# Windowed attention plus MLP on one core: GpSimd issues in written order, loads stand behind rstd and eight blocks ahead, and eight more q/k tiles are turned by DMA

## The chip, the core and the metric

The kernel runs on one core of a Trainium2 chip. The metric is the device time of one execution in microseconds. Three runs of the kernel before took 316.97, 318.75 and 320.42 us, median 318.75 us. One further execution was profiled. The core has TensorE (PE; its weight loads are shown apart as PEld), VectorE (DVE), ScalarE (ACT), GpSimd (POOL) and SyncE (SP), and 16 DMA engines. POOL and SP start DMAs from queues of their own: POOL's are the ones whose descriptors are made in software, and they can change the type on the way (fp32 to fp16 here); SP's also do transposes.

## What is computed

The reference, cut to what matters (8 batches, 8 heads, 576 positions, head size 64; model width 512, hidden width 2048):

```python
rel = pos[:, None] - pos[None, :]
bias = slopes[:, None, None] * (-np.abs(rel))[None]
mask = (rel >= 0) & (rel < 128)
scores = np.where(mask, scale * q @ k.T + bias, -1e9)
attn = softmax(scores)
x = (attn @ v).transpose(0, 2, 1, 3).reshape(B, S, 512)
xn = (x - mean(x)) / sqrt(var(x) + 1e-6) * g_ln
out = x + np.maximum(xn @ w_ch1, 0) @ w_ch2
```

## The kernel before, in words

**Blocks.** The 8 batches are taken as 4 pairs. Pair p has nine blocks of 128 positions: blocks 0 to 7 alternate between the two batches (four blocks of 128 positions each), and block 8 holds the 64 last positions of both. Through the whole kernel they are counted as n = 9p + block, 0 to 35. So block 4 of the second pair (p = 1) is n = 13. A block sees its own keys and those of the same batch one step back (two blocks back in n).

**Turns.** q and k come from memory with positions on the partitions, and the scores need the head dimension there. One *turn* (`turn`, L303 to L338) does that for q and k of two neighbouring blocks, or of block 8 alone: index i = block // 2 runs over 0 to 4. For pairs 0 to 2 PE does it, with 64 small transposes of 64x64 (32 for i = 4, L301) into the two score banks (or, for a few early turns, other banks), and DVE and ACT copy q and k out (L333, L334, L338). For pair 3 four DMA transposes on the SP queue do it (two for i = 4, L322). `turn_at(n)` places a turn three blocks ahead of its block when PE does it and four blocks ahead when DMA does it, and it is called with n + 1 at the end of step n.

After a PE turn both score banks hold leftovers (`junk`). The next scores into each bank then compute whole 64x128 tiles for one of the two head rows (`seen`, L395 on) where half of a tile would do.

**Steps.** From block 8 on, the step of block n does: the masks and values (probabilities times v, L489) of n, then the scores of n + 2 and their exponential on ACT (L436, L445), the mask products of later blocks on DVE (L456), the statistics of block n (`stats`: L586 and L587 on DVE, then two GpSimd instructions L541 and L544 that give rstd), a turn, and the normalised block xc on DVE (`normal`, L528), which waits for rstd. xc is turned into xT by a DMA transpose on the SP queue (L536). The first eight blocks get their statistics and centring another way, on DVE and PE alone.

**MLP.** Blocks are put in groups: six of two blocks, then six of four. `mlp1` (L732, ReLU on ACT L748 or DVE L740) and `mlp2` (L765 for the small groups; L831 for the big ones, which use a Strassen-like scheme with combinations on DVE, L800, L189) run on PE, and the steps of the blocks are woven between their units by hand (`weave_at`). The output adds are L909 and L849, the stores L924 and L928 on the SP queue.

**Loads.** q, k, v and the weights are loaded by GpSimd (L155, L196, L237, L234, L247), from one list in block order. For a PE turn (L237) a batch's q or k comes in one DMA with two positions side by side, so a run holds 128 elements; for a DMA turn (L234) k comes in one DMA per batch and q in two (even and odd positions apart), and a run holds 64 elements. `load_until(place[n + AHEAD])` lets the list run up to block n + 6 at the first half of the values of block n. There are four buffers each for raw q, raw k, turned q and turned k, ten for v.

**Order.** PE, SP, ACT and DVE run in the order in which the code writes their instructions (`manual_schedule`). GpSimd is not in that list before: its instructions are put in order by a scheduler at build time. In the program built that way the loads stand further ahead than six blocks at times, and loads stand in front of rstd, for instance q and k of blocks 20 and 21 around the rstd of block 9.

Of the kernel before, what the change touches and what calls it, by code (L numbers as in the profile page):

```python
# [26 lines left out]
FAST, HURRIED = 6, 11  # L27

NV = 10
BY_DMA_TURN = 3  # L30
AHEAD = 6

FIRST_GROUPS, FIRST = 2, 4

BY_DMA = SEEN = 8
# [24 lines left out]
def kernel(  # L60
# [146 lines left out]

    raw = {}

    def by_dma(p):  # L210
        return p >= BY_DMA_TURN

    def load_qk(src, tag, p, i):

        n = min(P, S - i * P)
        t = raw_pool.tile([P, H, 2, D], FP16, tag=tag, name=tag)
        raw[tag, p, i] = t
        if by_dma(p):
            t = raw[tag, p, i] = t.rearrange("p h r d -> p (h r d)").rearrange(
                "p (b h d) -> p b h d", b=2, h=H  # L220
            )
            for b in range(2):
                rows = src[2 * p + b, :, i * P : i * P + n, :]
                if i == 4:
                    parts = [(t[b * n : (b + 1) * n, 0], rows)]
                elif tag == "k":
                    parts = [(t[:, b], rows)]
                else:
                    rows = rows.rearrange("h (c r) d -> h r c d", r=2)
                    parts = [  # L230
                        (t[r * HALF : (r + 1) * HALF, b], rows[:, r]) for r in range(2)
                    ]
                for dst, part in parts:
                    nc.gpsimd.dma_start(out=dst, in_=part.rearrange("h p d -> p h d"))  # L234
            return
        for b in range(2):
            nc.gpsimd.dma_start(  # L237
                out=t[b * n // 2 : (b + 1) * n // 2],
                in_=src[2 * p + b, :, i * P : i * P + n, :].rearrange(
                    "h (c r) d -> c h r d", r=2  # L240
                ),
            )
# [10 lines left out]
    order = [(p, blk) for p in range(NPAIR) for blk in range(NSLOT)]  # L253
    w1s, w2s = ([(f, c) for c in range(4)] for f in (load_w1, load_w2))
    weights = {3: w1s + w2s[:2], 5: w2s[2:]}
    loads, place = [], []
# [21 lines left out]
    def warm(n):  # L278

        if n:  # L280
            ps = ps_mm.tile([P, 4 * P], FP32, tag="mm", name="ps_warm")
        for _ in range(n):
            nc.tensor.matmul(ps, ones[:, 0:P], ones, start=True, stop=True)  # L283
# [7 lines left out]
    def transposed(tag, p, i, ps):  # L291


        st = raw.pop((tag, p, i))
        for hp in range(HP):
            for r in range(2):
                for b, dst in enumerate(ps):
                    rows = slice(b * HALF, (b + 1) * HALF)
                    for j in range(2):
                        cols = slice(j * HALF, (j + 1) * HALF)  # L300
                        nc.tensor.transpose(  # L301
                            dst[cols, r, hp, :],
                            st[rows, 2 * hp + j, r, :],  # L303
                            iden[rows, rows],
                        )

    def turn(p, i, in_sc=False, copies=(nc.vector.tensor_copy, nc.scalar.copy)):

        k = keys_tile("k", p, i)
        q = queries(p, i) if i < 4 else keys_tile("q", p, i)
        if by_dma(p):
            for tag, dst in (("q", q), ("k", k)):
                src = raw.pop((tag, p, i))
                for b in range(2 if i < 4 else 1):
                    t = dst[:, b]
                    if tag == "q" and i < 4:  # L320
                        t = turned["q", p, i][:, b].rearrange("p h r c -> p h (r c)")
                    nc.sync.dma_start_transpose(  # L322
                        out=t, in_=src[:, b].rearrange("p h d -> p (h d)")
                    )
            return
        ps = [bank(b if in_sc else None) for b in range(2)]
        if i < 4:
            transposed("q", p, i, [t[:, 0] for t in ps])
            if p == 0 and i == 1:
                warm(3)  # L330
            transposed("k", p, i, [t[:, 1] for t in ps])
            for b, copy in enumerate(copies):
                copy(out=q[:, b], in_=ps[b][:, 0])  # L333
                copy(out=k[:, b].rearrange("p h (c r) -> p r h c", r=2), in_=ps[b][:, 1])  # L334
        else:
            for tag, t, dst, copy in zip("qk", ps, (q, k), copies):
                transposed(tag, p, i, [t[:, 0]])
                copy(out=dst[:, 0].rearrange("p h (c r) -> p r h c", r=2), in_=t[:, 0])  # L338

    def bank(sc=None):  # L340
        if sc is None:
            return ps_mm.tile([P, 2, 2, HP, HALF], FP16, tag="mm", name="ps_tr")
        junk[sc] = True
        return ps_sc[sc][:, 0].bitcast(FP16).rearrange(
            "p (t r h c) -> p t r h c", t=2, r=2, h=HP
        )

    def queries(p, i):
        if by_dma(p):
            t = turned_pool.tile([P, 2, HP, 2, HALF], FP16, tag="q", name="q")  # L350
            turned["q", p, i] = t
            return t
        t = turned_pool.tile([P, 2, 2, HP, HALF], FP16, tag="q", name="q")
        turned["q", p, i] = t.rearrange("p b r h c -> p b h r c")
        return t

    def keys_tile(tag, p, i):
        t = turned_pool.tile([P, 2, HP, P], FP16, tag=tag, name=tag)
        turned[tag, p, i] = t
        return t  # L360
# [259 lines left out]
    for g, size in enumerate(GROUPS):  # L620
        n = sum(GROUPS[:g])
# [3 lines left out]
    count = len(order)  # L625
# [5 lines left out]
    def scores_step(n):  # L631
        return [(scores,) + order[n]]

    def values_steps(n):
        p, blk = order[n]
        ahead = place[min(n + AHEAD, count - 1)]
        return [
            [(load_until, ahead), (masks, p, blk), (values, p, blk, 0)],
            [(values, p, blk, 1), (centre, p, blk)],
        ]  # L640

    def x_step(n, copy=nc.vector.tensor_copy):
# [6 lines left out]
    def masks_of(n, *halves):  # L649
        return [(masks,) + order[n] + halves]  # L650

    def warm_step(n):
        return [[(warm, n)]]


    steps = warm_step(11) + [[(turn_first,)]] + warm_step(3)
# [27 lines left out]
    def turn_at(n):  # L684
        ahead = [m for m in (n + 3, n + 4) if m < count and order[m][1] % 2 == 0]
        return [
            f
            for m in ahead
            if by_dma(order[m][0]) == (m == n + 4)
            for f in turn_step(m, True)  # L690
        ]

    steps.append(turn_at(8))
    for n in range(8, count):
        first_half, second_half = values_steps(n)
        step = first_half + second_half[:1]
        if n + 1 < count and order[n + 1][1] == T:
            step += [(scores_tail, order[n][0])]
        if n + 2 < count:
            step += scores_step(n + 2)  # L700
        steps.append(step)
        to_mask = [m for t in (n + 1, n + 2) if t < count for m in masks_of(t)]
        turns = [turn_at(n + 1)] if n + 1 < count else []
        if n == HURRIED:
            steps += [[(normal, n - 1)], to_mask + [(stats, n)], [(normal, n)], *turns]
        else:
            steps += [to_mask + [(stats, n)], *turns]
            if n != HURRIED - 1:
                steps.append([(normal, n)])
    combined = combine_w2()  # L710
# [236 lines left out]
    decay(m_tail, 4)  # L947
    load_until(place[3])
    engine = mybir.EngineType
    with tc.manual_schedule(engines={engine.PE, engine.SP}):  # L950
        with tc.manual_schedule(engines={engine.Activation, engine.DVE}):
            advance_to(first)
            weave_at(mlp1(0, (0, 1)), 2, 7, 8, 9, 13)
            weave_at(mlp1(1), 2, 8, 12)
            weave_at(mlp2(0, ((0, 8), (8, 12), (12, NFB))), 0, 1, 3, 4, 4, 5)
            weave_at(mlp2(1), 0, 1, 2, 3, 4, 6, 6)
            weave_at(mlp1(2), 0, 3, 3, 6, 8, 11)
            weave_at(mlp2(2), 0, 2, 4, 6, 7)


            weave_at(mlp1(3, (9, 10, 11)), 8, 8, 12, 15)
            weave_at(mlp2(3), 0, 1, 1, 3, 4, 4, 6, 6)
            weave_at(mlp1(4), 0, 4, 8, 10, 10, 14)
            weave_at(mlp2(4), 0, 2, 2, 5, 5, 7, also=(1, 4, 6))
            weave_at(mlp1(5), 0, 5, 5, 8, 10, 12, also=(3, 6, 9))
            weave_at(mlp2(5), 0, 1, 2, 4, 6, 7)
            ring += [ps_mm.tile([P, DM], FP32, tag="mm", name="ps_r") for _ in range(4)]
            for g in range(6, len(GROUPS)):
                weave_at(
                    mlp1(g), 0, 2, 5, 7, 8, 10, 13, 15, also=(1, 4) if g == 6 else ()  # L970
                )
                weave_at(fast_mlp2(g), 1, 3, 6, 7, 7, 10, 12, 13)
# [31 lines left out]
```

## Time and profile before

| | |
|---|---|
| runs, median (lowest to highest) | 318.75 us (316.97 to 320.42) |
| the profiled execution: its time | 317.64 us |
| its span | 315.8 us |
| granted PE clock, mean | 0.996 |
| busy: PE, DVE, ACT, POOL | 304.8, 228.8, 179.7, 125.8 us |
| PE transposes of q and k, L301, mean of one | 195 ns (overlapping) |
| copies of a turn: q and k on DVE (L333, L334) | 418 and 725 ns |
| copies of a turn: q and k on ACT (L333, L334) | 587 and 743 ns |
| load by POOL for a PE turn (L237), issue of one | 692 ns, x4 a turn |
| load by POOL for a DMA turn (L234), issue of one | q 708 ns x4, k 888 ns x2 |
| DMA transpose on SP (L322, L536), issue of one | 1.2 us |
| packets in the software queue, share of 16 engines | 89280, 74.1% |

The time is the span plus what lies around it (1.84 us here). Busy time of an engine is the union of its instructions; small PE instructions overlap, so a row's mean times its count is more than what it adds to PE. A line number is that of the kernel before. In the prediction's excerpts each row of the timeline gives the start, the length, the engine, the line, the operation and the count, and in brackets the idle time of the engine before it with what ended it.

### The profile page before, as it was taken

Reading aid. Unit: us, or ns where it says so; the run is one execution under the profiler, and the core shown is the slowest. Engines: PE = TensorE matmul, PEld = TensorE weight load, DVE = VectorE, ACT = ScalarE, POOL = GpSimd, SP = SyncE. Lnnn points to the kernel's source line nnn. Section 1 sums busy time; section 2 is a strip of 40 time slices with the busy share of each in tenths; the row PEclk is TensorE's granted clock in tenths of the full one; section 3 lists DMA queues with packets and bytes.
Section 4 is the critical chain, followed back from the end, with each engine's and each line's share of the span. In section 5 each row is a group of like instructions: output and inputs, shape, how many; then the busy total and the mean of one; then the engine's idle time right before and its main releaser. Section 6 shows DMA issues by size and latency. Waiting matters only on the chain.

```text
span 315.8 us, 9932 instructions
## 1 busy us (share of the span) xinstructions
PE 304.8 (97%) x4195; PEld 205.2 (65%) x4195; DVE 228.8 (72%) x547; ACT 179.7 (57%) x311; POOL 125.8 (40%) x198
## 2 busy tenths in 40 slices
PE   8989999999999999999999999999999999999994
PEld 2468655756757567554885488558756875784583
DVE  2788877877578698758994889479948994761363
ACT  6588765667667557378348832772487247305600
POOL 8932758666254356575254672140001001100001
PEclk9999999999999999999999999999999999999998
DMA  9999999999997999599959995892457144015004
GB/s 111 172 206 198 191 141 179 198 134 144 105 119 96 91 114 141 60 166 46 69 63 166 159 119 69 133 153 52 94 97 114 18 85 85 19 37 114 0 2 134
DMA packets 121087, 34.68 MB, mean 110 GB/s; under 512 B 112049, under 2 KB 116657, under 8 KB 121042
## 3 DMA queue, kind: packets, MB, share of 16 engines
q0 software_dynamic: 89280, 18.49, 74.1%
q1 hardware_dynamic: 31362, 15.09, 25.0%
q8 instruction: 33, 0.54, 0.7%
q10 hardware_dynamic: 400, 0.46, 0.5%
q14 instruction: 12, 0.10, 0.1%
HBM read 36.90 MB, written 9.44 MB: 147 GB/s over the span
## 4 chain that ended last, share of the span: by engine, by line
PE 84%; DVE 6%; ACT 4%; issue 2%; DMA 1%; POOL 1%; DVEq 0%; ACTq 0%
PE ps_r L732 27%; PE ps_r L831 23%; PE ps_m L732 10%; PE ps_m L765 9%; PE ps_sc L436 4%; PE ps_sc L301 3%; PE ps_r L489 3%; PE ps_warm L283 2%; PE ps_pv L489 2%; ACT probs L445 2%; DMA q<-in_q_dram 1%; DVE x L498 1%; DVE o L909 1%; DVE probs L456 1%; DVE o L849 1%
## 5 line engine op out<-in xcount | busy, mean ns | idle before, releaser
L732 PEld LDWEIGHTS <-w1g 128*128 128x128 f16 x640 | 60.4, 98 | 50.1 <-issue 1.9
L732 PE MATMUL ps_r<-xT,w1g 128*128 128x512 f16 x384 | 85.1, 379 | 0.0
L445 ACT ACTIVATE probs<-ps_sc 128x1024 f16<-128x1024 f32 x56 | 54.2, 1026 | 51.1 <-PE ps_sc L436 51.1
L748 ACT ACTIVATE ht<-ps_r 128x512 f16<-128x512 f32 x96 | 56.2, 600 | 31.6 <-PE ps_r L732 31.5
L541 POOL TENSOR_TENSOR rstd<-moments,powers 128x1 f32<-128x1 f32 x28 | 6.9, 245 | 99.1 <-DVE moments L587 98.1
L765 PE MATMUL ps_m<-w,ht 128*128 128x512 f16 x192 | 46.0, 380 | 0.0
L247 POOL DMA_DIRECT2D vx<-in_v_dram x40 | 34.5, 876 | 26.3 <-PE ps_r L489 9.0
L831 PE MATMUL ps_r<-w,ht 128*128 128x256 f16 x384 | 44.1, 273 | 0.0
L456 DVE TENSOR_TENSOR probs<-probs,m 128x1024 f16<-128x1024 f16 x56 | 37.5, 688 | 7.2 <-ACT probs L445 7.0
L831 PEld LDWEIGHTS <-ht 128*128 128x128 f16 x384 | 37.1, 98 | 4.8
L748 ACT ACTIVATE ht<-ps_m 128x256 f16<-128x256 f32 x91 | 33.3, 390 | 8.8 <-PE ps_m L732 6.2
L732 PE MATMUL ps_m<-xT,w1g 128*128 128x256 f16 x256 | 31.3, 273 | 1.9 <-DVE o L909 0.7
L765 PEld LDWEIGHTS <-ht 128*128 128x128 f16 x192 | 17.0, 98 | 17.5
L237 POOL DMA_DIRECT2D q<-in_q_dram x30 | 20.6, 693 | 16.0 <-PE ps_sc L301 8.6
L586 DVE BATCH_NORM_STATS2 st<-x 128x6 f32<-128x512 f16 x36 | 24.7, 685 | 0.0
L237 POOL DMA_DIRECT2D k<-in_k_dram x30 | 20.1, 681 | 5.6 <-DMA w<-in_moe_w_ch_dram 3.0
L436 PE MATMUL ps_sc<-q,k 64*64 64x128 f16 (+1 forms) x1088 | 20.7, 209 | 1.5 <-ACT probs L445 1.0
L831 PE MATMUL ps_r<-w,hs 128*128 128x256 f16 x192 | 21.9, 273 | 0.0
L489 PEld LDWEIGHTS <-probs 128*128 128x128 f16 x448 | 18.8, 97 | 4.7 <-DVE probs L456 0.3
L831 PEld LDWEIGHTS <-hs 128*128 128x128 f16 x192 | 18.8, 98 | 2.2
L849 DVE TENSOR_TENSOR o<-ps_r,o 128x512 f32<-128x512 f32 (+1 forms) x25 | 16.1, 655 | 5.0 <-PE ps_r L831 4.9
L528 DVE TENSOR_SCALAR xc<-x,moments,rstd 128x512 f16<-128x512 f16 x28 | 12.0, 428 | 10.4 <-POOL rstd L544 10.3
(89 smaller groups left out, 386.1 us busy)
## 6 DMA issues: line engine op xcount, KB each, us to landing
out_dram<-o SPq DMA_DIRECT2D x66, 128.0 KB, 2.5
k<-in_k_dram POOLq DMA_DIRECT2D x32, 128.0 KB, 6.0
vx<-in_v_dram POOLq DMA_DIRECT2D x32, 128.0 KB, 6.5
w<-in_moe_w_ch_dram POOLq DMA_DIRECT2D x8, 512.0 KB, 10.9
q<-in_q_dram POOLq DMA_DIRECT2D x24, 128.0 KB, 5.0
q<-in_q_dram POOLq DMA_DIRECT2D x24, 64.0 KB, 3.9
k<-in_k_dram POOLq DMA_DIRECT2D x8, 64.0 KB, 4.9
vx<-in_v_dram POOLq DMA_DIRECT2D x8, 64.0 KB, 6.3
```

The source lines that it names most:

```text
L237: nc.gpsimd.dma_start(out=t[b * n // 2 : (b + 1) * n // 2], in_=src[2 * p + b, :, i * P : i * P + n, :].rearrange("h (c r) d -> c h r d", ...
L247: nc.gpsimd.dma_start(out=vx[p0 : p0 + n, :, 0:D], in_=v[b, :, t0 : t0 + n, :].rearrange("h p d -> p h d"),)
L436: nc.tensor.matmul(in_halves(ps[cols, j, n, t, :])[:, r, queries], kt[rows, hp, cols], in_halves(qt[rows, b, hp])[:, r, queries], start=Tr ...
L445: nc.scalar.activation(out=dst.rearrange("p (n j) q -> p j n q", j=2), in_=ps.rearrange("p j n t q -> p j n (t q)"), func=AF.Exp, scale=in ...
L456: nc.vector.tensor_tensor(out=dst, in0=dst, in1=mask, op=ALU.mult)
L489: nc.tensor.matmul(ps[:, i, :], pr[:, h, t, :], vext[(p * NSLOT + o) % NV][:, h, :], start=(n == 0), stop=(n == len(terms) - 1),)
L586: nc.vector.bn_stats(out=st, in_=xs[order[n]])
L732: nc.tensor.matmul(ps[:, 0:cols], w[:, kb, fb * P : (fb + 1) * P], xT[:, kb, 0:cols], start=(kb == 0), stop=(kb == NKB - 1),)
L748: nc.scalar.activation(out=ht[:, fb, 0:cols], in_=ps[:, 0:cols], func=AF.Relu)
L765: nc.tensor.matmul(sums[at], ht[:, fb, at * P : (at + 1) * P], w2[:, fb, :], start=(fb == 0), stop=(fb == NFB - 1),)
L831: nc.tensor.matmul(banks[name][pair][:, pair, :], lhs[:, fb, pair * P : (pair + 1) * P], rhs[:, fb, :], start=(first and fb == 0 and (pair ...
L849: nc.vector.tensor_tensor(out=o[:, at, cols], in0=banks[name][at.start][:, at, :], in1=(x if to_x else o)[:, at, cols], op=ALU.add,)
```

## The change

```diff
-BY_DMA_TURN = 3
-AHEAD = 6
+BY_DMA_TURN = (1, 2)
+AHEAD = 8
...
-    def by_dma(p):
-        return p >= BY_DMA_TURN
+    def by_dma(p, i):
+        return (p, i) >= BY_DMA_TURN
...
+    def load_step(n):
+        return [(load_until, place[min(n + AHEAD, count - 1)])]
+
     def values_steps(n):
         p, blk = order[n]
-        ahead = place[min(n + AHEAD, count - 1)]
         return [
-            [(load_until, ahead), (masks, p, blk), (values, p, blk, 0)],
-            [(values, p, blk, 1), (centre, p, blk)],
+            [(masks, p, blk), (values, p, blk, 0)],
+            [(values, p, blk, 1), (centre, p, blk)] + load_step(n) * (n < BY_DMA),
         ]
...
-            if by_dma(order[m][0]) == (m == n + 4)
+            if by_dma(order[m][0], order[m][1] // 2) == (m == n + 4)
...
+        stats_step = [(stats, n)] + load_step(n)
...
-            steps += [to_mask + [(stats, n)], *turns]
+            steps += [to_mask + stats_step, *turns]
...
-    with tc.manual_schedule(engines={engine.PE, engine.SP}):
+    with tc.manual_schedule(engines={engine.PE, engine.SP, engine.Pool}):
```

The other places that ask `by_dma` (`load_qk`, `turn`, `queries`) pass i as well, and the step of block 11 (HURRIED) uses `stats_step` too.

Three things follow. GpSimd issues its instructions as written. The loads stand behind rstd of block n (behind the values, for the first eight blocks) and run up to block n + 8. And the turns of n = 13, 15, 17 (pair 1) and 18, 20, 22, 24, 26 (pair 2), eight in all of which two (17 and 26) are half size, are done by DMA transposes and loaded in 64-element runs.

More of the change, by code (lines that the diff above doesn't have):

```diff
@@ L217, in load_qk @@
         raw[tag, p, i] = t
-        if by_dma(p):
+        if by_dma(p, i):
             t = raw[tag, p, i] = t.rearrange("p h r d -> p (h r d)").rearrange(
@@ L314, in turn @@
         q = queries(p, i) if i < 4 else keys_tile("q", p, i)
-        if by_dma(p):
+        if by_dma(p, i):
             for tag, dst in (("q", q), ("k", k)):
@@ L348, in queries @@
     def queries(p, i):
-        if by_dma(p):
+        if by_dma(p, i):
             t = turned_pool.tile([P, 2, HP, 2, HALF], FP16, tag="q", name="q")
@@ L702 @@
         to_mask = [m for t in (n + 1, n + 2) if t < count for m in masks_of(t)]
+        stats_step = [(stats, n)] + load_step(n)
         turns = [turn_at(n + 1)] if n + 1 < count else []
         if n == HURRIED:
-            steps += [[(normal, n - 1)], to_mask + [(stats, n)], [(normal, n)], *turns]
+            steps += [[(normal, n - 1)], to_mask + stats_step, [(normal, n)], *turns]
         else:
-            steps += [to_mask + [(stats, n)], *turns]
+            steps += [to_mask + stats_step, *turns]
             if n != HURRIED - 1:
```

## The prediction, made before the changed kernel ran

> **What bounds the kernel now.** I read the page's slices first.
>
> ```profile
> span 315.8 us, 9932 instructions
> ...
> PE   8989999999999999999999999999999999999994
> ...
> PEclk9999999999999999999999999999999999999998
> DMA  9999999999997999599959995892457144015004
> ```
>
> PE is busy in nearly every slice at full clock, so a microsecond of PE work removed is worth a microsecond, and a transfer counts only when it makes PE wait. The DMA row stays at nine up to about 190 us: the weak point of a change that adds DMA work. Next, busy time in stretches of 10 us (length; PE, PEld, DVE, ACT, POOL; clock; DMA packets in flight per engine; GB/s).
>
> ```profile
> 60.00:70.00 10.00, 9.45 (x188) 6.19 (x186) 7.25 (x27) 5.86 (x13) 7.21 (x10) 1.00 2.35 152
> ...
> 90.00:100.00 10.00, 9.01 (x163) 5.97 (x162) 8.47 (x21) 6.38 (x13) 2.65 (x6) 1.00 0.93 119
> 100.00:110.00 10.00, 9.75 (x145) 6.64 (x146) 7.18 (x17) 6.86 (x13) 5.33 (x8) 1.00 0.93 97
> 110.00:120.00 10.00, 9.67 (x200) 6.68 (x198) 9.68 (x21) 6.08 (x13) 5.79 (x10) 1.00 1.08 120
> ...
> 170.00:180.00 10.00, 10.00 (x120) 5.16 (x119) 6.10 (x13) 8.06 (x13) 3.59 (x7) 1.00 1.80 179
> ```
>
> From 130 to 309 us PE has no idle time at all; between 90 and 130 us it has a little. Last, PE in order of time, around the turns.
>
> ```profile
> 85.96 0.45 PE L301 MATMUL ps_sc<-iden,q 64*64 64x64 f16 x32
> 86.22 0.45 PE L301 MATMUL ps_sc<-iden,k 64*64 64x64 f16 x32
> 86.60 1.90 PE L765 MATMUL ps_m<-w,ht 128*128 128x512 f16 x8
> ...
> 95.05 1.16 PE L732 MATMUL ps_m<-xT,w1g 128*128 128x256 f16 x8 [0.63 <-DVE x L498]
> 96.58 2.78 PE L732 MATMUL ps_m<-xT,w1g 128*128 128x256 f16 x24 [0.37 <-DVE o L909]
> ...
> 101.39 0.63 PE L436 MATMUL ps_sc<-q,k 64*64 64x128 f16 x32
> 101.96 1.92 PE L732 MATMUL ps_m<-xT,w1g 128*128 128x256 f16 x16
> 104.13 0.60 PE L732 MATMUL ps_m<-xT,w1g 128*128 128x256 f16 x4 [0.25 <-ACT ht L748]
> ...
> 107.73 0.54 PE L436 MATMUL ps_sc<-q,k 64*64 64x128 f16 x32
> 108.20 2.76 PE L765 MATMUL ps_m<-w,ht 128*128 128x512 f16 x12
> ```
>
> A turn holds PE from its first start to the next instruction's start (85.96 to 86.60, 0.64 us). The scores after a turn take 0.57 us (101.39 to 101.96), others 0.47 us (107.73 to 108.20). The brackets are PE's stalls.
>
> **Term 1, the transposes: -5.1 us.** The eight turns begin at 85.96, 99.29, 110.90, 117.85, 130.11, 144.99, 161.66 and 176.74 us. They hold PE for 0.64, 0.64, 0.62, 0.64, 0.64, 0.65, 0.64 and 0.62 us: 5.09 us, all on the path.
>
> **Term 2, narrower scores: -0.65 us.** No leftovers in the banks, so the seven slow scores behind these turns (such as 101.39) lose 0.09 us each; the half of own-block scores I count as nothing more.
>
> **Term 3, stalls between 90 and 130 us: -1.3 us, bounds +2.5 and -1.9.** PE idles 0.63, 0.37, 0.25, 0.33 (before 115.34) and 0.31 us (before 123.33): 1.89 us. Each has a removed cause. The first two come from DVE, late because xc of block 9 waited until 90.28 us for rstd. The chain shows why:
>
> ```profile
> 86.73 0.43 POOL q L237
> ...
> 88.14 0.68 POOL k L237
> 88.82 0.22 POOL rstd L541
> 89.04 0.06 POOL k L237
> ...
> 89.66 0.60 POOL rstd L544
> ```
>
> The statistics were ready at 87.45; the loads for blocks 20 and 21 stood ahead of both halves of rstd. In written order rstd comes first, at 88.3 us instead of 90.25. The stalls of 0.25 and 0.31 wait for ReLU on ACT, behind two copies of a turn (0.59 + 0.74 us), which go. The stall of 0.33 waits for an output add on DVE behind a q copy of 0.73 us and combinations of w2; the copy goes.
>
> What can come instead: now rstd of block n+1 stands behind the loads of block n+8. A full load step is 4 x 0.71 (q) + 2 x 0.89 (k) + 0.92 (v) = 5.5 us, with rstd itself (0.26 + 0.56) 6.4 us. The rstd pairs in the timeline start at 94.56 (block 10), 98.63 (11), 105.43 (12), 111.79 (13), 118.49 (14) and 124.74 (15). Full steps follow 10, 12 and 14, so waits of 2.3, 0 and 0.1 us; with intervals some 1 us shorter after the removals (and 10 to 11 unchanged), 2.3, 1.0 and 1.1: 4.4 us of DVE waiting. At worst all reaches PE (4.4 in place of 1.89, +2.5 us). Queued behind the waiting xc on DVE are the reciprocal and scaling of the next values, which free PE's two banks of four. After block 11's xc that work arrived 1.7 us later anyway (99.48 + 0.41 to 101.26), so I pass 0.6 us to PE: 1.89 - 0.6 = 1.3. Past 130 us such waits are free: xc at 140.23 waited 1.84 us for rstd and PE stayed at 10.00 of 10.
>
> **What is added, and its cover.** Removed copies (14 on DVE, 14 on ACT) lie off the path apart from term 3. POOL gets 12 more q DMAs and longer k issues, 6 x (4.6 - 2.8) = 11 us of 126 busy; covered by its idle time but for the rstd waits above. SP gets 28 transposes of 1.2 us, 34 us. xT stands in the same queue, but a turn needs only its load and a freed buffer and SP can take it early: turn 13 needs loads issued near 50 to 56 us and stands behind the stores that end at 77.1 us, so it occupies 77 to 82; xT of block 8 was issued at 82.6. Turns 15, 18, 20 and 24 I place the same way near 91, 110, 121 and 151 us, each two or more us before the next xT is ready. With landings of 5.2 us at worst (range of L322, 2.4 to 5.2), turn 18 lands near 120 us, its scores start at 126.94 - 4.5 = 122.4: the least slack, 2 to 3 us. Cost 0, at most 3 us if that cover goes. v loads never wait long: the slot of block n + 8 is that of n - 2, read last by the values of n, already done.
>
> **xT landings: 0, bound +2.7 us.** xT of a group's last block starts at 90.7, 106.8, 126.0, 158.3, 190.2 and 220.4 us for groups 4 to 9, and their mlp1 at 93.83, 114.40, 134.52, 166.07, 197.09 and 227.11: slacks of 3.1, 7.6, 8.5, 7.8, 6.9 and 6.7 us. For group 4 the earlier rstd makes about 4.2. Landings of xT range from 2.4 to 6.8 us. If all took 6.8, groups 4 and 9 would lose 2.6 and 0.1. I take 0, since near 89 us only a half-size load is issued and the row there is 3.0 us.
>
> **Sum.** 5.1 + 0.65 + 1.3 = 7.05 us. On the profiled execution 317.64 - 7.05 = 310.6; that run is 1.1 us below the median, so for the median 318.75 - 7.05 = 311.7 us.
>
> **Rivals.** *A, transfers fall behind; slower.* Loads in 64-element runs double their packets: a full turn has 2 tensors x 2 batches x 8 heads x 64 = 2048 runs before, so six turns x 2048 + two x 1024 = 14,300 more on 89,280. At 0.741 x 315.8 x 16 / 89,280 = 42 ns a packet that is 38 us per engine. The 28 transposes take up to 40 us more (at most 580 of the hardware queue's 31,362 packets each, at 40 ns). Packets in flight between 75 and 190 us go from about 1.25 to 1.8; if landing times rise alike, 6.8 becomes 9.9 us, and groups 4 to 9 lose 5.7, 2.3, 1.4, 2.1, 3.0 and 3.2 = 17.7 us: 329.4 us. It turns the sign once all xT landings pass 8 us (3.8 + 0.4 + 0 + 0.2 + 1.1 + 1.3 = 6.8). For it: DMA nines. Against: at 2.35 in flight (60 to 70 us) q and k loads still landed in a median of 5.6 us, and 170 to 180 us already holds all three kinds of traffic at 1.80 with xT at 5.1 to 5.5. 8%.
> [...]
>
> *B, GpSimd's order gives the stalls back.* All 4.4 us of rstd waits reach PE: 5.1 + 0.65 - 2.5 = 3.2, so 315.5 us. For: four banks shared by values and mlp1, and a stall of just this kind at 95 us. Against: DVE sheds 4 us of copies there. 16%.
>
> *C, turns do not leave the path:* scores wait about 1 us on each of most DMA turns: no change, 318.7. Against: in pair 3 nothing of the kind is seen, PE is at 10.00. 4%.
>
> **How the numbers follow.** Forecast 72%: 311.7, its own range 309 to 315. Low end: every stall gone, also 0.56 and 0.41 us at 62 and 73 us, 8.6 us off the lowest run (316.97): 308.4, rounded to 308.5. High end takes in B: 316. A and C stay out. About 1% is what a measurement here can tell from no change: 315.6 and below is faster. Faster: 0.72 + half of B = 0.80; same: half of B + C = 0.12; slower: A, 0.08.
>
> **What would show it.** L301 falls by 448 matmuls and PE busy by about 5.7 us; POOL rstd for block 9 is no longer behind q and k; the stalls at 95, 96 and 104 us are gone or short; PE idles nowhere after 130 us; xT lands within 7 us. I am wrong if mlp1 (L732) or scores (L436) are seen waiting for a DMA, or DVE's xc waits for rstd grow and PE's stalls between 90 and 130 us exceed 1.9 us.

## The result and the profile after

| | before | after |
|---|---|---|
| median of 6 runs on one chip | 317.72 us | 315.68 us |
| lowest to highest | 316.97 to 320.42 us | 312.16 to 319.96 us |
| profiled execution: time, span | 317.64, 315.8 us | 315.53, 313.8 us |
| profiled execution: PE busy, granted clock | 304.8 us, 0.996 | 300.4 us, 0.987 |

The ratio is 0.9898, with an interval of 0.9856 to 0.9939: about 1% or 3.2 us faster. It leaves out two runs of the changed kernel (317.88 and 319.96) that count as slow, so it lies below the quotient of the medians. The medians themselves are 2.0 us apart. The time is inside the range on record, 308.5 to 316.0, 0.3 us below its top: the gain is less than half of the 7.05 us that the sum gave.

The head of the page and three rows of its 40 slices (7.8 us each), of the changed kernel:

```profile
span 313.8 us, 9068 instructions
...
PE   8989999999999999699999999999999999999994
...
PEclk9999999999999999969999999999999999999999
DMA  9999999999799999990999999999945043015004
```

One digit of PE has become a 6, the 17th (125.5 to 133.4 us), and the next slice has a 6 in the clock row. In the page of before both rows are nines there. The same place in finer stretches (length; PE, PEld, DVE, ACT, POOL busy with counts; clock; DMA packets in flight per engine; GB/s):

```profile
90.00:130.00 40.00, 37.71 (x527) 25.36 (x525) 30.65 (x74) 22.85 (x45) 29.59 (x45) 1.00 1.88 161
130.00:131.00 1.00, 0.00 (x0) 0.00 (x0) 0.61 (x3) 0.79 (x1) 1.00 (x2) 1.00 7.31 129
131.00:132.00 1.00, 0.00 (x0) 0.00 (x0) 1.00 (x2) 0.00 (x0) 1.00 (x2) 0.91 0.26 20
132.00:138.00 6.00, 5.16 (x13) 1.86 (x14) 1.89 (x5) 1.19 (x2) 3.04 (x5) 0.50 1.98 215
138.00:139.00 1.00, 1.00 (x5) 0.40 (x4) 0.00 (x0) 0.60 (x1) 0.00 (x0) 0.68 1.45 215
...
145.00:300.00 155.00, 155.00 (x1675) 105.75 (x1674) 113.78 (x241) 79.85 (x119) 51.05 (x80) 1.00 0.93 97
```

PE does nothing from 129.7 to 132.8 us, and then runs at half clock until 138.7 us. Before and after that nothing dramatic happens: from 90 to 130 us it is busy 37.71 of 40 us (38.13 before), with 0.3 us of the hole among the difference; from 145 to 300 us all the time, as before. PE in order of time, first after, then before:

```profile
129.29 0.41 PE L436 MATMUL ps_sc<-q,k 64*64 64x128 f16 x16
132.84 9.93 PE L735 MATMUL ps_r<-xT,w1g 128*128 128x512 f16 x32 [3.13 <-DMA xT<-xc]
142.60 0.42 PE L489 MATMUL ps_r<-vx,own 128*128 128x65 f16 x8
```

```profile
134.17 0.41 PE L436 MATMUL ps_sc<-q,k 64*64 64x128 f16 x16
134.52 7.08 PE L732 MATMUL ps_r<-xT,w1g 128*128 128x512 f16 x32
141.43 0.42 PE L489 MATMUL ps_r<-vx,own 128*128 128x65 f16 x8
```

The 32 matmuls are the start of mlp1 for group 6. PE is free for them at 129.7 us in place of 134.5, so 4.8 us had been won. It waits 3.13 us for xT, takes 9.93 instead of 7.08 us for the same matmuls, and leaves them at 142.60, 1.17 us behind the kernel before. All that had been won up to there is lost in this one place. With the three turns that go after it the kernel is ahead again: mlp1 of group 9 starts at 195.72 us in place of 197.09.

The xT that it waits for is that of block 15. First SP's own instructions in the changed kernel, then the one on DVE that makes xc of block 15:

```profile
116.18 1.20 SPq L536 DMA_TRANSPOSE xT<-xc  x1
117.91 2.06 SPq L931 DMA_DIRECT2D out_dram<-o  x2
120.07 1.27 SPq L536 DMA_TRANSPOSE xT<-xc  x1
121.52 2.66 SPq L322 DMA_TRANSPOSE q<-q  x2
124.28 2.52 SPq L322 DMA_TRANSPOSE k<-k  x2
126.90 1.22 SPq L536 DMA_TRANSPOSE xT<-xc  x1
```

```profile
122.84 0.41 DVE L528 TENSOR_SCALAR xc<-x,moments,rstd 128x512 f16<-128x512 f16 x1 [1.53 <-POOL rstd L544]
```

xc of block 15 is ready at 123.25 us, and its transpose is issued at 126.90: for 3.65 us it stands behind the four transposes of turn 20, which no matmul needs yet. The chain of waits then goes through its landing (start, length, what):

```profile
126.90 5.89 DMA xT<-xc
...
132.84 9.93 PE ps_r L735 x32
```

So xT lands 3.65 us of queue and 5.89 us of landing after xc is ready, and PE, free 6.45 us after xc, waits for the rest. (xT of block 13, issued at 116.18, had stood 5.2 us behind turn 18 in the same way; nothing waited for it.) The profile shows this much. What the experiments had to settle: whether SP's order or the slower landing decides, whether the half clock belongs to the wait, and what each half of the change is worth alone.

### The profile page after: what moved, and what is told of

The parts are those of the page before. It is cut to its first block, busy times and chain, and to the rows that moved or that the text cites. A ratio compares the mean times of both kernels' runs of the same rounds, so it can differ in the third digit from the quotient of the medians.

```text
span 313.8 us, 9068 instructions
## 1 busy us (share of the span) xinstructions
PE 300.4 (96%) x3747; PEld 200.8 (64%) x3747; DVE 220.6 (70%) x533; ACT 171.7 (55%) x297; POOL 140.0 (45%) x210
## 4 chain that ended last, share of the span: by engine, by line
PE 73%; POOL 8%; DVE 8%; DMA 6%; issue 2%; ACT 1%; POOLq 0%; DVEq 0%
PE ps_r L735 28%; PE ps_r L834 23%; PE ps_m L768 7%; PE ps_m L735 6%; DMA w<-in_moe_w_ch_dram 4%; PE ps_sc L436 4%; PE ps_r L489 3%; DMA xT<-xc 2%; DVE probs L456 2%; POOL vx L247 2%; POOL q L234 1%; DVE x L498 1%; POOL rstd L544 1%; DVE st L586 1%; POOL k L234 1%
## 5 line engine op out<-in xcount | busy, mean ns | idle before, releaser
L735 PEld LDWEIGHTS <-w1g 128*128 128x128 f16 x640 | 61.3, 99 | 55.9 <-issue 4.8
L735 PE MATMUL ps_r<-xT,w1g 128*128 128x512 f16 x384 | 87.6, 389 | 3.1 <-DMA xT<-xc 3.1
L541 POOL TENSOR_TENSOR rstd<-moments,powers 128x1 f32<-128x1 f32 x28 | 8.0, 286 | 111.9 <-DVE moments L587 111.7
L768 PE MATMUL ps_m<-w,ht 128*128 128x512 f16 x192 | 45.5, 380 | 0.0
L234 POOL DMA_DIRECT2D q<-in_q_dram x46 | 32.4, 714 | 0.7 <-DMA vx<-in_v_dram 0.5
L497 DVE RECIPROCAL rec<-ps_r 128x4 f32<-128x4 f32 x36 | 6.3, 175 | 25.3 <-PE ps_r L489 25.3
L234 POOL DMA_DIRECT2D k<-in_k_dram x26 | 22.2, 871 | 0.2
L436 PE MATMUL ps_sc<-q,k 64*64 64x128 f16 (+1 forms) x1088 | 19.9, 208 | 1.6 <-ACT probs L445 1.0
L528 DVE TENSOR_SCALAR xc<-x,moments,rstd 128x512 f16<-128x512 f16 x28 | 11.9, 426 | 12.6 <-POOL rstd L544 10.7
```

What stands on the lines that cost most here:

```text
L436: nc.tensor.matmul(in_halves(ps[cols, j, n, t, :])[:, r, queries], kt[rows, hp, cols], in_halves(qt[rows, b, hp])[:, r, queries], start=Tr ...
L528: nc.vector.tensor_scalar(out=xc, in0=xs[order[n]], scalar1=moments[:, n, 0:1], scalar2=rstd[:, n : n + 1], op0=ALU.subtract, op1=ALU.mult,)
L735: nc.tensor.matmul(ps[:, 0:cols], w[:, kb, fb * P : (fb + 1) * P], xT[:, kb, 0:cols], start=(kb == 0), stop=(kb == NKB - 1),)
L768: nc.tensor.matmul(sums[at], ht[:, fb, at * P : (at + 1) * P], w2[:, fb, :], start=(fb == 0), stop=(fb == NFB - 1),)
```

## The experiments

The kernel before was run beside each set of variants; a ratio is against those runs of it. The chip differs from set to set, so kernels of different sets are compared by their ratios.

**The turn behind the next xT.** In all steps but block 10's:

```diff
+            late = []
+            if turns and any(by_dma(p, i) for _, p, i, *_ in turns[0]) and n != HURRIED - 1:
+                late, turns = turns[0], [[]]
             steps += [to_mask + stats_step, *turns]
             if n != HURRIED - 1:
-                steps.append([(normal, n)])
+                steps.append([(normal, n)] + late)
```

> Only the SP queue's order differs from the changed kernel: each DMA turn stands behind the xT transpose of its step instead of ahead of it (the turn of block 15 alone keeps its place). Theory (SP order: xT of block 15 waits for the four transposes of the turn of block 20, PE idles 3.1 us at the first mlp1 of four blocks and then runs 2.9 us slower at a granted clock of 0.66): xT of block 15 is issued about 3.5 us sooner, the stall and the low clock go, 309 to 310.5 us. Rival (the DMA engines are behind, xT lands late wherever it stands): the stall stays at 2 us or more, 314 to 316 us. Second rival (xc of block 15 itself is late because its rstd stands behind loads): the stall shrinks by less than half, 313 to 315 us.

Measured: 311.97 us, ratio 0.9815 (0.9789 to 0.984). Two rows of PE in its timeline:

```profile
93.94 4.96 PE L738 MATMUL ps_m<-xT,w1g 128*128 128x256 f16 x44 [1.58 <-DMA xT<-xc]
...
130.52 7.07 PE L738 MATMUL ps_r<-xT,w1g 128*128 128x512 f16 x32 [0.37 <-DVE rec L497]
```

The wait for xT at group 6 is gone and the low clock with it. The time is still above the 309 to 310.5 us expected, and the same kind of wait appears at group 4: turn 13 now stands between xT of block 8 and xT of block 9 on SP (83.46 to 88.65, xT of block 9 at 88.76), and PE waits 1.58 us for the second. One profile does not show that the new place causes it: the changed kernel, profiled again below, waits 1.22 us for the same xT with turn 13 in its old place. A later run puts turn 13 back.

**Only the half clock taken away.** Fifteen matmuls without use, on ones, fill PE's wait in front of group 6; everything else is the changed kernel.

```diff
+            keep_busy(15)
             for g in range(6, len(GROUPS)):
```

> The changed kernel with 15 matmuls of 128x512 (3.2 us at full clock) on ones put ahead of the first mlp1 of four blocks, into a bank that is overwritten next; the output is unchanged. Theory (the low clock comes from the idle time): PE is busy while xT of block 15 is on its way, the granted clock stays at 1.00 between 130 and 140 us, and the 2.9 us of slow matmuls go: 312 to 313 us. Rival (the clock drops for another reason): 0.66 again, 315 to 317 us.

Measured: 312.82 us, ratio 0.9854 (0.9831 to 0.9877). The fill-in matmuls and those of group 6 on PE, and the stretch that ran at half clock:

```profile
129.72 3.41 PE L289 MATMUL ps_r<-ones 128*128 128x512 f16 x15
132.97 7.07 PE L741 MATMUL ps_r<-xT,w1g 128*128 128x512 f16 x32
```

```profile
132.00:138.00 6.00, 6.00 (x30) 2.71 (x28) 1.96 (x5) 2.90 (x5) 3.12 (x5) 1.00 1.86 205
```

xT lands no earlier (issued at 126.50, landing 6.3 us, so at 132.8 us; in the changed kernel 126.90 + 5.89 = 132.8), but with PE occupied the clock stays at 1.00 and the 32 matmuls take 7.07 us. In the profiled runs the wait is paid nearly twice, once as 3.13 us of idle time and once as 9.93 - 7.07 = 2.9 us of slow matmuls after it. The times show less of it: between the ratio of this kernel and those of the changed kernel (0.9898, and 0.9913 below) lie 1.4 to 1.9 us. Not every execution of the changed kernel gets the low clock: its run with a mean granted clock of 1.000 took 312.16 us, no more than the runs of this kernel (312.20 to 313.69).

**The turns alone:** the kernel before, with its scheduler's order on GpSimd and loads six blocks ahead, but the same eight turns by DMA.

```diff
-BY_DMA_TURN = 3
+BY_DMA_TURN = (1, 2)
...
-    def by_dma(p):
-        return p >= BY_DMA_TURN
+    def by_dma(p, i):
+        return (p, i) >= BY_DMA_TURN
```

> The kernel before with the eight turns by DMA alone: GpSimd still in the scheduler's order, six blocks ahead. Theory (SP order): the turn of block 20 stands ahead of xT of block 15 here too, so PE waits 1 to 4 us for that xT; 312 to 316 us. Rival (GpSimd's written order is what makes xT late): no such wait, 310 to 311.5 us.

Measured: 338.2 us, ratio 1.0653 (1.0626 to 1.068): 21 us slower, beyond everything expected. Its table of waits (engine, line, waited for: us in total, times, longest) and GpSimd in order of time:

```profile
DVE xc L528 <- POOL rstd L544: 43.6, 13, 7.7
POOL q L234 <- DMA q<-q: 43.3, 9, 6.4
```

```profile
87.28 2.74 POOL L234 DMA_DIRECT2D q<-in_q_dram  x4 [4.57 <-DMA q<-q]
90.00 0.24 POOL L541 TENSOR_TENSOR rstd<-moments,powers 128x1 f32<-128x1 f32 x1
90.90 0.93 POOL L234 DMA_DIRECT2D k<-in_k_dram  x1 [0.66 <-DMA k<-k]
91.83 0.58 POOL L544 TENSOR_TENSOR rstd<-rstd,powers 128x1 f32<-128x1 f32 x1
```

A load's buffer is now freed by the DMA transpose that reads it. GpSimd waits for that transpose in the load, and rstd, which PE needs soon, stands behind the waiting load in the same queue. The waits of DVE for rstd grow from 10.3 us (kernel before) to 43.6. Over the whole change they stay at 10.7, so GpSimd's written order is not a second improvement beside the turns: without it they cost 21 us. (This kernel also loads six blocks ahead, not eight; what that is worth comes below.)

**The order alone:** the changed kernel with pairs 0 to 2 turned by PE.

```diff
-BY_DMA_TURN = (1, 2)
+BY_DMA_TURN = (3, 0)
```

> The changed kernel with pairs 0 to 2 turned by PE as before: only GpSimd's order and the distance of the loads are changed. Theory: the two stalls behind rstd of block 9 (1.0 us) go, and rstd of blocks 11 and 13 behind loads gives back half of it or more; no wait for xT; 317 to 318 us. Rival (the order is the main gain): 315 us or less. Rival (the order is the main loss): 319 us or more.

Measured: 315.76 us, ratio 0.9957 (0.9938 to 0.9975), 1.4 us faster, more than the theory gave and less than its rival. All stalls of PE from 90 to 130 us in its timeline:

```profile
103.52 0.60 PE L735 MATMUL ps_m<-xT,w1g 128*128 128x256 f16 x4 [0.25 <-ACT ht L751]
...
114.72 2.58 PE L735 MATMUL ps_m<-xT,w1g 128*128 128x256 f16 x20 [0.31 <-DVE o L912]
...
122.69 1.47 PE L735 MATMUL ps_m<-xT,w1g 128*128 128x256 f16 x12 [0.31 <-ACT ht L751]
```

0.87 us of the 1.89 are left: the two behind the late rstd of block 9 (0.63 and 0.37) are gone, those put down to the copies of turns stay, since here the copies stay. The loss that the theory set against this, from rstd behind loads, did not come.

**The turn behind xT after block 11 only** (the first edit with `n > HURRIED` for `n != HURRIED - 1`), so that block 8's xT and block 9's stay together:

> Each DMA turn behind the xT of its step from block 12 on only; the turn of block 13 stands ahead of xT of block 8 as in the changed kernel. Theory (the order on SP decides, place by place): the wait of 1.58 us for xT of block 9, which the version with all turns behind xT showed at 94 us, falls back to the changed kernel's 0.8 us behind DVE, and there is no wait for xT of block 15: about 311.2 us, 0.5 to 1 us below that version. Rival (the order at blocks 8 and 9 does not matter): 312 us.

Measured: 309.66 us, ratio 0.9755 (0.9727 to 0.9783), the lowest median of all the versions, 7.5 us faster than before. PE at group 6, and SP:

```profile
129.55 7.07 PE L738 MATMUL ps_r<-xT,w1g 128*128 128x512 f16 x32 [0.18 <-DMA xT<-xc]
```

```profile
119.63 4.52 SPq L536 DMA_TRANSPOSE xT<-xc  x2
124.32 2.50 SPq L322 DMA_TRANSPOSE q<-q  x2
```

xT of blocks 14 and 15 leave one after the other, the second ending its issue at 124.15, and turn 20 follows. No matmul up to 150 us waits for the delayed turn. Against the version with all turns behind xT, the ratios give turn 13's place 1.9 us, where 0.5 to 1 us was expected: a turn only helps behind an xT where it isn't pushed in front of another. The two profiled spans are 0.9 us apart (308.6 and 307.7), with a wait at group 4 of 0.39 us here in place of 1.58; the rest stays open.

**The same, with the loads of q and k split over two steps** (q of block n + 9 issued with v of n + 8, so that rstd waits behind fewer at once):

```diff
-        return [(load_until, place[min(n + AHEAD, count - 1)])]
+        m = min(n + AHEAD, count - 1)
+        early = n >= BY_DMA and m + 1 < count and order[m + 1][1] % 2 == 0
+        return [(load_until, place[m] + early)]
```

> As the version with turns behind xT from block 12 on, and each full load step is split: the q of block n+9 is issued with the v of block n+8, so that rstd stands behind at most 3.8 us of loads instead of 5.5. Theory (rstd waits behind loads cost PE part of their length): the wait of xc of blocks 13 and 15 for rstd falls by more than 1 us each, the PE stalls between 110 and 120 us (0.8 and 0.3 us) shrink to half or less: 310 to 310.8 us. Rival (DVE's own work sets these stalls): the same time as without the split, within 0.4 us.

Measured: 310.31 us, ratio 0.9781 (0.975 to 0.9813), not told apart from the one above. The longest wait of DVE for rstd, at block 11, shrank from 3.18 to 0.94 us; PE's stalls from 90 to 130 us are 0.58, 0.83, 0.29, 0.58 and 0.26, 2.5 us, no less than the 0.39, 0.56, 0.78, 0.25 and 0.18 without the split. Those waits do not set PE's stalls.

**Six blocks ahead** (the changed kernel with AHEAD = 6):

> The changed kernel with loads six blocks ahead instead of eight. Theory: a turn on SP is written five blocks ahead, so its load is issued one block (some 6 us) before it; the issue of the load (5.5 us) and its landing (5 us) take longer, SP waits in front of xT, and PE waits for several xT: 320 to 330 us. Rival (eight blocks are not needed): 315 to 316 us.

Measured: 316.06 us, ratio 0.9955 (0.9926 to 0.9983). The ratios put it 1.3 to 1.8 us behind the changed kernel, at the edge of what these runs tell apart. Turn 20 again stands in front of xT of block 15 (issued at 129.26), and PE shows a hole at the same place, 3.81 us before 134.83, with the 32 matmuls at 8.77 us. The profile puts the end of this hole down to an operation of DVE (L189) that ended at 134.83; xT, with a landing of 5.5 us, came just before it, at 134.8. The 320 to 330 us of the theory did not come: loading eight blocks ahead is worth 2 us at most here, and perhaps nothing.

**The loads in front of rstd**, in written order:

```diff
-        stats_step = [(stats, n)] + load_step(n)
+        stats_step = load_step(n) + [(stats, n)]
```

> The changed kernel with the load of block n+8 ahead of rstd of block n instead of behind it. Theory: every second rstd comes up to 5.5 us after its statistics, xc and everything behind it on DVE wait, and PE's four banks run out between 90 and 130 us; xT of block 15 is later too: 319 to 326 us. Rival (DVE and PE take such waits without loss, as past 130 us in the kernel before): 315 to 317 us.

Measured: 317.97 us, ratio 1.0037 (1.0013 to 1.0062), between the two expectations. The stalls from 90 to 130 us change little. What grows is the hole:

```profile
137.51 9.89 PE L735 MATMUL ps_r<-xT,w1g 128*128 128x512 f16 x32 [6.77 <-DMA xT<-xc]
```

With the load issued first, its packets are in flight when xT follows (from 90 to 130 us 2.39 packets in flight per engine, in the changed kernel 1.88): landings of xT between 100 and 135 us have a median of 8.4 us, in the changed kernel 6.4, and xT of block 15, issued at 128.55, takes 8.9. Of the 3.6 us by which the hole is longer, 3.0 are the landing and 1.65 the later issue (128.55 for 126.90), less 1.0 us by which PE comes later (130.74 for 129.70). So where loads stand matters here mostly through the landing of xT.

**One turn alone:** only turn 20 goes behind xT of block 15 (the first edit with `n == 15`); run with the changed kernel again beside it.

> The changed kernel with one place altered on the SP queue: the turn of block 20 stands behind xT of block 15 instead of ahead of it. Theory (that one place holds nearly the whole loss): no wait for xT of block 15 above 0.5 us and no low clock, 309.5 to 310.5 us. Rival (turns ahead of xT cost something at every step, and 15 only happens to come last): 312 to 314 us, with waits for the xT of another group.

Measured: 310.21 us, ratio 0.9762 (0.9731 to 0.9792). PE's wait at group 6 is 0.33 us, and the profile puts it down to DVE:

```profile
130.76 7.07 PE L738 MATMUL ps_r<-xT,w1g 128*128 128x512 f16 x32 [0.33 <-DVE rec L497]
```

> The changed kernel itself, on the same chip as the version with one place altered. Theory: a wait for xT of block 15 of 2 us or more and a granted clock of 0.5 behind it in most executions, 314.5 to 317 us, and the spread of its times goes with the clock: those with a mean clock above 0.995 near 312 to 313 us.

Measured: 315.7 us, ratio 0.9913 (0.988 to 0.9946); its profiled run waits 3.92 us for xT at 133.40 us. The spread goes with the clock as expected: the one run with a mean clock of 1.000 took 312.84 us, the seven between 0.987 and 0.995 took 314.27 to 316.32, and one at 0.982 took 318.08. About five microseconds (5.5 by the medians, 4.8 by the ratios) hang on the place of four DMA issues. The landings of xT between 100 and 135 us are as slow with turn 20 moved (median 6.6 us) as without (6.4): the order on SP decides, and the slow landing alone does not.

## Why the prediction was right and where it was wrong

**The account.** Between the two profiled executions the span fell by 2.0 us. In the kernel with the turns behind xT, where the hole is absent, PE's busy time fell from 304.8 to 297.6, 7.2 us; in the changed kernel that is the same work, plus 2.85 us of half clock (9.93 - 7.08), plus the hole of 3.13 us, less 0.7 us of other idle time (idle is span less busy: 11.0 before, 13.4 after): -7.2 + 2.85 + 3.13 - 0.7 = -1.9. So the time came to lie within the range by luck: the range reached up to 316 for rival B, and what used up the room was the wait for xT, which stands in the sum at 0, and the half clock, which does not stand in it. Two of the forecast's own signs of being wrong came: mlp1 was seen waiting for a DMA, and, though only just, the waits for rstd grew (10.3 to 10.7 us) with PE's stalls between 90 and 130 us above 1.9 us (2.0).

**Terms 1 and 2** were right in kind and too small: 5.75 us forecast, 7.2 measured. The L301 groups fell by 448 matmuls as forecast, and scores behind a turn take 0.47 to 0.48 us. The groups named by the forecast account for most of it: L301 6.2 + 5.7 + 1.3 + 0.9 us before and 2.4 + 2.2 + 1.3 + 0.9 after, 7.3 less what overlaps between q and k, and L436 20.7 to 19.8, 0.9 in place of 0.65. The rest lies in small steps of the long matmul groups, such as L765 (46.0 to 45.5). That the turns no longer interrupt them would explain it, and a turn's price, read as its first start to the next instruction's start, leaves that out; no run tried it.

**Term 3** was wrong in size. The cause was right: rstd of block 9 starts at 87.05 in the changed kernel, not 88.82, and the order alone removes the two stalls behind it. But with the turns gone PE reaches the same DVE work earlier and waits there:

```profile
93.28 4.96 PE L735 MATMUL ps_m<-xT,w1g 128*128 128x256 f16 x44 [0.77 <-DVE x L498]
...
100.36 1.60 PE L735 MATMUL ps_m<-xT,w1g 128*128 128x256 f16 x12 [0.19 <-DVE x L498]
...
112.21 3.89 PE L735 MATMUL ps_m<-xT,w1g 128*128 128x256 f16 x32 [0.78 <-DVE o L912]
...
118.20 2.47 PE L735 MATMUL ps_m<-xT,w1g 128*128 128x256 f16 x20 [0.26 <-DVE x L498]
```

These four are 2.00 us, where 1.89 us of the kernel before were to shrink by 1.3. The waits for rstd did come where they were forecast (3.17 us at block 11, 2.3 forecast), but splitting the loads shrank them and left the stalls. That PE's earlier arrival at DVE's work makes them is what remains; no run tried that by itself.

**The step that failed** is the cover of the transposes on SP: "Turns 15, 18, 20 and 24 I place the same way near 91, 110, 121 and 151 us, each two or more us before the next xT is ready." The places were right (turns 18 and 20 came at 110.80 and 121.52). Two things in it were not. First, a turn begun two microseconds ahead (turn 20: 1.7 us before xc of block 15) does not clear the way: its four issues hold SP for 5.3 us, as the forecast itself had for turn 13 (77 to 82). Second, the slack of group 6, 134.52 - 126.0 = 8.5 us, is made of two times of the kernel before. The sum moved the first of them itself: with 4.8 us won by then, PE wants xT at 129.70. xc is early too (123.25), but behind turn 20 the transpose is issued at 126.90. Slack 2.8 us, landing 5.89, wait 3.1. Issued as soon as xc was ready, with the same landing, it would have landed at 123.25 + 5.89 = 129.14, before PE came. In the run with one turn moved it was issued near 124.0; with the median landing of that run, 6.6 us, it is there at 130.6, just before PE's matmuls at 130.76.

**The term that was not in the sum at all** is the half clock after the wait: 5.8 us at half clock (132.84 to 138.64) lose 2.9 us. The forecast read the clock row as full speed and priced idle time at its length. In the trace the granted clock began to fall near 131.8 us (0.91 from 131 to 132 us), 2.1 us into the idle time, was 0.50 from 132 to 138 us and came back near 138.6 (0.68 from 138 to 139 us). With the idle time filled by the fifteen matmuls it stayed at 1.00, and the 32 matmuls took 7.07 us for 9.93.

**Landings of xT** "0, bound +2.7", were too optimistic: between 100 and 130 us the median went from 3.5 to 6.4 us (4.7 to 6.4 if the stretch runs to 135 us) and the longest was 7.6. By itself that cost at most 0.3 us at group 6 (above), but it made the queue's 3.65 us count.

**The rivals.** A had the mechanism in part: packets as forecast (14,528 more in the software queue), in flight 1.02 to 1.88 from 90 to 130 us (but only 1.22 to 1.48 from 75 to 190, where it had 1.8), landings up by 1.8 times in the stretch to 130 us and by 1.4 times in that to 135. Its price of 17.7 us did not come, since the longest landing stayed below the 8 us from which it was to decide. B gave nearly the time that was measured (315.5), by another mechanism: the stalls from 90 to 130 us were to grow by 2.5 us and grew by 0.1, and the order alone gained 1.4. C fell with the 7.2 us of PE work. What came was none of them: an order on SP that spoils one transfer. Without that place the gain of 7.05 us would have come out (317.17 - 309.66 and 317.71 - 310.21, 7.5 us each), but as the sum of a first part that was 1.45 us too small and a third that was too large: that their errors cancel is luck.

## What to carry to other kernels

In a queue that issues in order, put what someone will wait for soonest ahead of what has slack, even where the second could go first: a transfer with slack is early for itself and late for all behind it (here xT of block 15 stood 3.65 us behind turn 20). When a change takes work off the bounding engine, recompute every slack with that engine's new times, not the old ones, and look for a low clock behind an idle time of that engine: here holes of 3.1 to 6.8 us were followed by 1.7 to 3.0 us of loss at half clock. Two halves of a change need not add: here turns alone cost 21 us, the order alone gained 1.4, both gained about 3, and both with one issue order swapped 7.5.

## What the runs showed of the hardware

In the traces of the changed kernel and of the turns alone the granted clock fell to 0.50 and came back about 3.4 or 6.8 us later. Here is the kernel with the turns alone (stretches of 1 us, columns as above):

```profile
92.00:93.00 1.00, 0.00 (x0) 0.00 (x0) 0.55 (x2) 0.00 (x0) 1.00 (x2) 1.00 0.91 53
...
94.00:95.00 1.00, 0.88 (x41) 0.76 (x42) 0.97 (x4) 0.11 (x1) 0.20 (x1) 1.00 1.01 73
95.00:96.00 1.00, 1.00 (x7) 0.30 (x4) 1.00 (x3) 1.00 (x2) 0.68 (x1) 0.61 1.61 160
...
98.00:99.00 1.00, 1.00 (x8) 0.76 (x7) 1.00 (x3) 0.43 (x2) 0.00 (x0) 0.68 1.52 216
...
122.00:123.00 1.00, 0.00 (x0) 0.00 (x0) 1.00 (x3) 0.00 (x0) 0.04 (x1) 0.77 0.82 138
```

A mean of 0.61 over a stretch in which the clock goes from 1.00 to 0.50 puts the fall at 95.22. In the same way it came back at 98.64, fell again at 122.54 and came back at 129.36 (0.66 from 128 to 130 us): gaps of 3.42, 23.90 and 6.82 us. In the changed kernel it fell at 131.82 and came back at 138.64, 6.82 us again. The length of one idle time alone does not decide a fall; what does was not shown. In the 3.42 us ahead of a fall PE was busy 1.3 us in the changed kernel, and 1.5 and 0.63 us with the turns alone, the last of them without an idle time above 1.9 us. Beside an idle time of 2.19 us (before 106.98) the clock stayed at 1.00 from 104 to 110 us. With the order alone its mean was 0.97 from 0 to 20 us and from 20 to 60 us, where the changed kernel has 1.00.

The fall can come late: after an idle time of 2.46 us (before 93.57) PE had been working again for more than a microsecond when the clock fell at 95.22. And the price does not follow the length of the hole. Behind holes of 3.13, 3.81, 3.92 and 6.77 us (the changed kernel, six blocks ahead, the changed kernel again, loads in front of rstd) the 32 matmuls of group 6 took 9.93, 8.77, 10.04 and 9.89 us, where 7.08 is the time at a granted clock of 1.00 (the kernel before).

How much of the slower landings comes from the 64-element loads, how much from the transposes and how much from where the loads stand was not taken apart. The medians between 100 and 135 us, of five to seven landings each, only order it: 4.7 us before, 4.3 with the turns alone (where other blocks fall into the stretch), 5.5 with the order alone, 6.4 with both, 5.4 with both and loads six blocks ahead, 8.4 with the load in front of rstd.
